# Clustered attention and a SwiGLU FFN on one core: two copies, two casts, two transposes and three weight loads change engine or place

## The chip, the cores and the metric

The kernel runs on one core of a Trainium2 chip. The core's engines work side by side, each through its own queue in order: TensorE (PE in the profile; PEld is its weight load), VectorE (DVE), ScalarE (ACT), GpSimd (POOL) and SyncE (SP), which issues DMAs. The metric is the device time of one execution in microseconds (us); of several executions the median is quoted.

## The reference

Batch 4, 8 heads, 768 tokens, head size 64; then a gated FFN from 512 to 1536 and back.

```python
q_assign = argmax(einsum('bhsd,hcd->bhsc', q_n, c_n))     # nearest of 16 centroids
k_assign = argmax(einsum('bhsd,hcd->bhsc', k_n, c_n))
mask = q_assign[:, :, :, None] == k_assign[:, :, None, :]
scores = where(mask, scale * q @ k.T, -1e9)
attn = softmax(scores)
x = (attn @ v) -> (tokens, heads * head size)
xn = x / sqrt(mean(x * x) + 1e-6) * rms_g
out = (silu(xn @ w_gate) * (xn @ w_val)) @ w_out
```

Each query attends only to keys of its own cluster.

## The kernel before, in words

**Tiling.** Tokens lie on 128 partitions. Work goes by units: a unit is one batch entry and one half of its queries (384), so there are 8 units of 8 heads. A head's scores take three steps of 384 queries by 256 keys, each followed by one exponential. A place (u, h, i) names unit, head and step; the steps of the first unit are also counted as gaps 0 to 23 (gap 3h + i). Heads are gathered in groups of four: group 0 is heads 0 to 3 of the first batch entry, group 1 heads 4 to 7, group 2 and 3 the next entry's.

**The mask.** Queries and keys are extended by 16 rows that hold the one-hot code of their cluster. A key's code is part of the product, so that scores of the same cluster rise by a large constant, which the exponential's bias takes away again; the others become zero.

**A head's preparation.** `trans` transposes a head's queries or keys on TensorE into a PSUM tile (`tq`), which VectorE or ScalarE copies to SBUF (`qkT`), as its argument says. `cast` turns one half of such a copy into bf16 in `qext` or `kext` (K0, K1, Q0, Q1 are the halves of keys and queries). `pair_clusters(p)` makes the one-hot codes of heads 2p and 2p + 1: products with the centroids on TensorE (`sc`), then a block transpose, a maximum and a comparison on VectorE (`scT`, `mx`, `pads`). `head(n)` lays head n's codes under keys and queries by two block transposes on VectorE (`under`). `vcast` turns a head's values into bf16 on GpSimd.

**Attention.** `scores` makes a step's products and its exponential on ScalarE (`pT`). `pv` multiplies a head's exponentials by its values. Two heads share one accumulator (`acc`, one buffer); behind the second of them VectorE divides by the row sums (`inv`, `x`), and only then may the next pair use the accumulator. In `attention`, step 1 of head h is followed by `pv` of head h - 1.

**Order.** The schedule is written by hand: what is emitted first stands first in its engine's queue. In the first unit the table `first` says what is emitted in which gap, behind that gap's scores and `pv`: gap 1 `gap1` (codes of heads 2 and 3, casts of heads 4 and 5), gaps 2 to 4 the transposes of heads 6 and 7 (`early`), gap 5 `gap5` (codes of heads 4 and 5, casts and value casts on GpSimd, two weight loads, at its end `head(4)`), gap 7 `head(5)`, gap 9 codes of heads 6 and 7, gap 10 `head(6)`, gap 13 the casts of head 6's keys and `head(7)`, from gap 15 transposes of group 2 (`late`). Gaps without an entry get `more`: one filler matmul (`warm`). All of `tq`, `sc`, `warm` and the FFN's products share one PSUM tag (`gen`) with three buffers, taken in turn.

In the second unit the FFN of the first one is mixed with the preparation of the next batch entry. `prep` is a list of such steps: `c` (value casts and loads), `a` (codes of group 2 and their placing by small DMAs on SP's queue), then transposes `t3` and casts `c3` of group 3, woven one by one; `spread` puts the three loads of the output weights `wo` (`o3`, on GpSimd's queue) evenly between them.

Of the kernel before, what the change touches and what calls it, by code (L numbers as in the profile page):

```python
# [22 lines left out]
def kernel(  # L23
# [12 lines left out]
    nc = tc.nc  # L36
# [48 lines left out]
    def load_qk(n):  # L85
        if n < B * H:
            load(n, 0)
            load(n, 1)

    def load_v(n, vq=None):  # L90
        if n >= B * H:
            return
        stagedv[n] = stage.tile([P, ST, D], F32, tag="vs", name="vs", bufs=NV)
        (vq or nc.sync).dma_start(out=stagedv[n], in_=src(v, n))
# [18 lines left out]
    def busy(n, first=True):  # L113
        to = ps_a.tile([P, 512], F32, tag="acc", name="warm") if first else \
            ps_g.tile([P, 512], F32, tag="gen", name="warm")
        for i in range(n):
            nc.tensor.matmul(to.rearrange("p (a b) -> p a b", b=P), lhsT=warm,  # L117
                             rhs=warm.unsqueeze(1).broadcast_to([P, 4, P]), start=True, stop=True)
# [72 lines left out]
    def load_gv(i):  # L191
        c = slice(i * DF // 4, (i + 1) * DF // 4)
        for w, of in ((wg, moe_w_gate), (wv, moe_w_val)):
            nc.gpsimd.dma_start(out=w[:, :, c], in_=of[:, c].rearrange("(c p) f -> p c f", p=P))

    def load_o(c):
        nc.gpsimd.dma_start(out=wo[:, c:c + 4], in_=moe_w_out[c * P:(c + 4) * P].rearrange("(c p) f -> p c f", p=P))
# [4 lines left out]
    def trans(g, h, part, on=None):  # L202
        if (g, h // 2) not in qkT:
            qkT[g, h // 2] = qk32.tile([P, 2, 2, UQ], F32, tag="qkT", name="qkT")
        qk = staged[g * HG + h]
        ps = ps_g.tile([P, UQ], F32, tag="gen", name="tq")
        for i in range(HT):
            nc.tensor.transpose(ps[:, i * P:(i + 1) * P], qk[:, part, 2 * i:2 * i + 2].rearrange("p t d -> p (t d)"),  # L208
                                ident_f)
        to, by = qkT[g, h // 2][:, h % 2, part], 1.0 / ZS if part else 1.0  # L210
        if on is nc.vector:
            nc.vector.tensor_scalar_mul(to, ps, by)
        else:
            nc.scalar.activation(to, ps, ACT.Copy, scale=by)  # L214
# [5 lines left out]
    def cast(on, g, h, part, es=(0, 1)):  # L220
        for e in es:
            to = cols((kext if part else qext)[g % 4][:D, h], g, e)
            of = qkT[g, h // 2][e * D:(e + 1) * D, h % 2, part]
            if on is nc.scalar:
                nc.scalar.copy(to, of)
            else:
                on.tensor_copy(to, of)  # L227

    def vcast(n):
        nc.gpsimd.tensor_copy(vbf[n // HG % 4][:, n % HG, :, :D], stagedv[n])  # L230
# [62 lines left out]
    def slot(n, m):  # L293

        return 32 * (2 * (n % 2) + m if n < 2 else 2 * m + n % 2)

    def pair_clusters(p, heads=(0, 1)):
        g, h = divmod(2 * p, HG)
        what = [(h + i, m) for i in heads for m in range(2)]
        at = [slot(2 * p + i, m) for i in heads for m in range(2)]  # L300
        r = slice(min(at), max(at) + 32)
        pool = ps_g if p else ps_s
        ps = pool.tile([P, UQ], F32, tag="gen" if p else "s", name="sc")
        for a, (hh, m) in sorted(zip(at, what)):
            nc.tensor.matmul(ps[a:a + 32], lhsT=cblk[:, g * HG + hh], rhs=qkT[g, hh // 2][:, hh % 2, m],
                             start=True, stop=True)
        sct = asg.tile([P, UQ], F32, tag="scT", name="scT", bufs=2)
        nc.vector.transpose(sct[r], ps[r])
        cl = sct[r].rearrange("p (b e c) -> p b e c", e=2, c=NC)
        mx = small.tile([P, NB, 2], F32, tag="mx", name="mx")[r]  # L310
        nc.vector.tensor_reduce(mx, cl, axis=AX, op=ALU.max)
        nc.vector.tensor_tensor(pads[p][r, :, :NC].rearrange("p b c e -> p b e c"), cl,  # L312
                                mx.unsqueeze(3).broadcast_to([mx.shape[0], NB, 2, NC]), op=ALU.is_equal)

    def under(n, m):
        i = slot(n, m)
        nc.vector.transpose((kext if m else qext)[n // HG][D:D + 32, n % HG].bitcast(I32),  # L317
                            pads[n // 2][i:i + 32].rearrange("p b c e -> p (b c e)").bitcast(I32))
# [181 lines left out]
    def weave(t, c):  # L500

        return [x for pair in zip(t, c) for x in pair] + c[len(t):]
# [5 lines left out]
    def spread(a, b):  # L508

        if not a:  # L510
            return list(b)
        w, n = [], 0
        for i, x in enumerate(a):
            w.append(x)
            while n < len(b) * (i + 1) // len(a):
                w.append(b[n])
                n += 1
        return w

    def ffn_work(u):  # L520
        n = UNITS[u][2] / HT
        w = [(0.18 * n, lambda c=c: xtrans(u, c)) for c in range(CC)]
        for f in range(FC):
            for val in (False, True):
                w.append((0.64 * n, lambda f=f, val=val: gv(u, f, val)))
        return w

    def out_work(u):
        return [(0.86, lambda t=t, p=p: out_mm(u, t, p)) for t in range(UNITS[u][2]) for p in range(3)]
# [10 lines left out]
    def head(n):  # L540
        under(n, 1)
        under(n, 0)

    def casts(on, n, *what):
        for m, e in what:
            cast(on, n // HG, n % HG, m, (e,))

    K0, K1, Q0, Q1 = (1, 0), (1, 1), (0, 0), (0, 1)
    pool_ = nc.gpsimd
# [32 lines left out]
    def more():  # L582
        busy(1, False)
# [3 lines left out]
    def second_batch():  # L587
        nc.sync.dma_start(out=hold, in_=invs[0].rearrange("p a t -> p (a t)"))
        for n in range(H + HG, H + NQ):
            load_qk(n)  # L590
        for n in range(H, H + NV):
            load_v(n)
# [13 lines left out]

    def gap5():
        pair_clusters(2)
        casts(pool_, 6, Q0)
        vcast(4)  # L610
        casts(pool_, 7, Q0)
        for n in (4, 5):
            casts(pool_, n, Q1)
        vcast(5)
        casts(pool_, 7, K0, K1)
        vcast(6)
        load_gv(2)
        vcast(7)
        for n in (6, 7):
            casts(pool_, n, Q1)  # L620
        load_gv(3)
        head(4)

    early = [lambda h=h, m=m: trans(1, h, m) for h in (2, 3) for m in (1, 0)]
    late = [lambda h=h, m=m: trans(2, h, m, nc.vector if h < 3 else None) for h in range(HG) for m in (1, 0)]
    first = {0: lambda: trans(1, 0, 0), 1: gap1, 2: early[0], 3: early[1], 4: lambda: (early[2](), early[3]()), 5: gap5,
             7: lambda: head(5), 9: lambda: pair_clusters(3), 10: lambda: head(6),
             13: lambda: (casts(nc.vector, 6, K0, K1), head(7)), 14: lambda: (more(), second_batch())}
    first.update({16: None, 19: None, 22: None})
    first.update({i: f for i, f in zip((15, 17, 18, 20, 21, 23), late)})  # L630

# [24 lines left out]
    for u in range(1, NU):  # L656
        ffn, o, g = ffn_work(u - 1), out_work(u - 2) if u > 1 else [], u + 2
        if u == 1:
            t, c, a = group_work(2)
            t3, c3, a3 = group_work(3)  # L660
            n = LEAD - 4
            o3 = [(0.0, lambda i=i: load_o(i)) for i in range(0, FC, 4)]
            prep = c + a + spread(weave(t3[n:], c3), o3) + a3[:5]
            idle = const.tile([P, 1], BF16)

            def norm():
                rms(0)
                nc.gpsimd.tensor_copy(idle, xn[0][:, HT - 1, DM - 1:])
                for h in range(HG):
                    casts(pool_, H + h, K0, Q0, K1, Q1)  # L670

            hooks = {(1, 0, 0): late[6], (1, 0, 1): lambda: (late[7](), norm())}
            hooks.update({(1, *divmod(2 + i, HT)): t3[i][1] for i in range(n)})
            hooks[1, *divmod(LEAD - 1, HT)] = lambda: xtrans_all(0)
            fill = spread(ffn[CC:CUT], prep)
            attention([(1, h) for h in range(H)], fill, LEAD, hooks)
        else:
            fill = ffn_work(u - 2)[CUT:] + [(0.0, lambda u=u: rms(u - 1))]
            fill += border(spread(o[:3], a3[5:]) + o[3:], ffn) if u == 2 else border(o, ffn)
            attention([(u, h) for h in range(H)], fill + spread(ffn[CC:CUT], group(g) if g < NG else []), 1)  # L680
# [41 lines left out]
```

The softmax here doesn't subtract the row's maximum and nothing guards it: scores larger than these inputs give would overflow.

## Time and profile before

| | us |
|---|---|
| median of 9 runs | 347.2 |
| lowest and highest | 347.05, 353.47 |
| the profiled execution, its time | 353.47 |
| its span | 351.7 |
| TensorE busy | 340.8 (97%) |
| ScalarE busy | 260.0 (74%) |
| VectorE busy | 221.3 (63%) |
| GpSimd busy | 113.0 (32%) |

The profiled execution is one of the nine, and the longest. Its span runs from the first to the last instruction; the remaining 1.8 us lie around it. Times in the text that name a moment are microseconds from the span's start.

The page gives busy time in 40 slices of 8.8 us, as tenths; the fourth row is the TensorE clock that was granted:

```profile
PE   8999999599999999999999999999999999999996
DVE  6999796748457745686457863677456653666330
ACT  5899979455787877887688877978778887764422
POOL 6999596210542702444033711427000000000000
PEclk9999999879999999999999999999999999999999
```

The first four slices are the first attention unit. The eighth slice (62 to 70 us) is the only one before the last where TensorE is much less than full, and the clock is lower there and in the slice behind it.

### The profile page before, as it was taken

The page shows a single profiled execution, that of the slowest core. Times are in us where ns is not written, and L with a number is a line of the kernel's source. Part 1 is how long each engine was busy: PE and PEld are TensorE (multiplying, and loading weights), DVE is VectorE, ACT ScalarE, POOL GpSimd, SP SyncE. Part 2 cuts the span into 40 slices and gives each one's busy share as a digit, 9 for nine tenths or more (in the row PEclk, how much of TensorE's full clock was granted, in tenths as well). Part 3 has the DMA queues.
Part 4 walks back from the last instruction along what each step waited for, and adds up shares of the span by engine and source line. Part 5 has one row for each costly group of instructions (what it writes and reads, how often), then busy time and mean ns, then how long its engine had stood idle before and what let it go on. Part 6 is the DMA issues. An engine that isn't in the chain of part 4 may idle for free.

```text
span 351.7 us, 7999 instructions
## 1 busy us (share of the span) xinstructions
PE 340.8 (97%) x3045; PEld 209.6 (60%) x3045; DVE 221.3 (63%) x540; ACT 260.0 (74%) x449; POOL 113.0 (32%) x225
## 2 busy tenths in 40 slices
PE   8999999599999999999999999999999999999996
PEld 4547657264665656655576556756566656665654
DVE  6999796748457745686457863677456653666330
ACT  5899979455787877887688877978778887764422
POOL 6999596210542702444033711427000000000000
PEclk9999999879999999999999999999999999999999
DMA  7999979762262012610130011000010001001002
GB/s 277 372 200 209 267 146 235 122 213 100 71 183 90 23 62 91 187 34 17 60 122 2 17 38 60 2 2 23 32 62 0 2 31 62 2 1 62 30 2 89
DMA packets 27302, 31.62 MB, mean 90 GB/s; under 512 B 4480, under 2 KB 24320, under 8 KB 27264
## 3 DMA queue, kind: packets, MB, share of 16 engines
q1 hardware_dynamic: 18608, 25.02, 21.6%
q0 software_dynamic: 8368, 5.71, 10.1%
q8 instruction: 24, 0.39, 0.5%
q10 hardware_dynamic: 288, 0.39, 0.3%
q14 instruction: 14, 0.11, 0.1%
HBM read 28.35 MB, written 6.29 MB: 98 GB/s over the span
## 4 chain that ended last, share of the span: by engine, by line
PE 82%; ACT 6%; DVE 5%; DMA 5%; issue 1%; POOL 0%; ACTq 0%; DVEq 0%; POOLq 0%
PE o L448 17%; PE gate L423 16%; PE val L423 16%; PE s L333 15%; PE acc L351 9%; ACT pT L337 4%; PE tq L208 4%; PE sc L241 2%; DMA kext<-oh 2%; DMA qk<-in_q_dram 2%; PE tx L396 1%; PE warm L117 1%; DVE pads L312 1%; DVE kext L317 1%; DVE qext L317 1%
## 5 line engine op out<-in xcount | busy, mean ns | idle before, releaser
L337 ACT ACTIVATE pT<-s,off 128x768 bf16<-128x768 f32 x192 | 170.9, 905 | 38.7 <-PE s L333 37.9
L333 PE MATMUL s<-qext,kext 80*128 80x384 bf16 x384 | 95.0, 329 | 5.8 <-DMA kext<-oh 3.9
L432 DVE SCALAR_TENSOR_TENSOR th<-th,gate 128x384 f32<-128x384 f32 x84 | 46.4, 552 | 54.3 <-ACT th L431 54.2
L423 PE MATMUL gate<-xnT,wg 128*128 128x384 bf16 x384 | 79.3, 328 | 0.5 <-DVE gvT L436 0.4
L423 PE MATMUL val<-xnT,wv 128*128 128x384 bf16 x384 | 78.8, 328 | 0.0
L448 PE MATMUL o<-wo,gvT 128*128 128x512 bf16 x276 | 67.4, 379 | 0.0
L227 POOL CAST qext<-qkT 64x384 bf16<-64x384 f32 x64 | 35.4, 559 | 76.2 <-ACT qkT L214 67.9
L333 PEld LDWEIGHTS <-kext 80*128 80x128 bf16 x384 | 36.5, 98 | 36.3 <-issue 11.1
L431 ACT ACTIVATE th<-gate 128x384 f32<-128x384 f32 x84 | 41.2, 491 | 15.5 <-PE gate L423 15.1
L423 PEld LDWEIGHTS <-wv 128*128 128x128 bf16 x384 | 36.3, 98 | 25.6 <-issue 4.3
L423 PEld LDWEIGHTS <-wg 128*128 128x128 bf16 x384 | 36.2, 98 | 25.6 <-issue 4.5
L436 DVE SCALAR_TENSOR_TENSOR gvT<-th,val 128x384 bf16<-128x384 f32 x84 | 46.2, 550 | 6.5 <-PE val L423 2.0
L351 PEld LDWEIGHTS <-pT 128*128 128x128 bf16 x1152 | 43.9, 98 | 10.2 <-DVE x L358 1.1
L351 PE MATMUL acc<-vbf,pT 128*128 128x65 bf16 x1152 | 46.2, 194 | 0.6 <-ACT pT L337 0.2
L448 PEld LDWEIGHTS <-gvT 128*128 128x128 bf16 x276 | 25.8, 97 | 25.1
L208 PE MATMUL tq<-ident_f,qk 128*128 128x128 f32 x192 | 31.2, 282 | 0.1
L214 ACT ACTIVATE qkT<-tq 128x384 f32<-128x384 f32 x57 | 26.9, 495 | 4.2 <-PE tq L208 3.7
L282 POOL DMA_DIRECT2D qext<-oh x40 | 19.2, 488 | 30.6 <-DVE oh L271 30.6
L397 DVE TENSOR_SCALAR xnT<-tx,gcol 128x384 bf16<-128x384 bf16 x28 | 10.5, 412 | 28.8 <-PE tx L396 28.8
L208 PEld LDWEIGHTS tq<-ident_f,qk 128*128 128x128 f32 x192 | 24.0, 145 | 6.8 <-ACT qkT L214 1.0
L451 ACT COPY o_sb<-o 128x512 f32<-128x512 f32 x23 | 13.5, 586 | 17.4 <-PE o L448 17.4
L282 POOL DMA_DIRECT2D kext<-oh x40 | 19.1, 487 | 15.8 <-DVE oh L271 15.8
(81 smaller groups left out, 247.9 us busy)
## 6 DMA issues: line engine op xcount, KB each, us to landing
qk<-in_q_dram SPq DMA_DIRECT2D x32, 192.0 KB, 3.7
vs<-in_v_dram SPq DMA_DIRECT2D x32, 192.0 KB, 4.0
out_dram<-o_sb SPq DMA_DIRECT2D x23, 256.0 KB, 2.0
qk<-in_k_dram SPq DMA_DIRECT2D x30, 192.0 KB, 3.9
wg<-in_moe_w_gate_dram POOLq DMA_DIRECT2D x4, 384.0 KB, 8.6
wv<-in_moe_w_val_dram POOLq DMA_DIRECT2D x4, 384.0 KB, 10.8
wo<-in_moe_w_out_dram POOLq DMA_DIRECT2D x3, 512.0 KB, 9.2
qext<-oh POOLq DMA_DIRECT2D x40, 12.0 KB, 1.6
```

The costliest lines, as they stand in the source:

```text
L208: nc.tensor.transpose(ps[:, i * P:(i + 1) * P], qk[:, part, 2 * i:2 * i + 2].rearrange("p t d -> p (t d)"), ident_f)
L214: nc.scalar.activation(to, ps, ACT.Copy, scale=by)
L227: on.tensor_copy(to, of)
L282: on.dma_start(out=ext[D:D + NC, h, e * UQ:(e + 1) * UQ], in_=put[g, m][32 * h + e * NC:32 * h + (e + 1) * NC])
L333: nc.tensor.matmul(ps[:, j, :w] if nt == HT else flat[:, j * w:(j + 1) * w], lhsT=cols(kext[g % 4][:KR, hh], g, kc // HT, kc % HT * P, (kc ...
L337: nc.scalar.activation(pT[u, h][:, n * i:n * i + n, :w], of, ACT.Exp, bias=off, scale=scale * ZS)
L351: nc.tensor.matmul(acc[:, h % 2, t], lhsT=pT[u, h][:, kc, t * P:(t + 1) * P], rhs=vbf[g % 4][:, hh, kc % HT * 2 + kc // HT], start=kc == 0 ...
L423: nc.tensor.matmul(ps, lhsT=w[:, c, f * P:(f + 1) * P], rhs=xnT[u][:, c, :n], start=c == 0, stop=c == CC - 1)
L431: nc.scalar.activation(th, ps, ACT.Tanh, scale=0.5)
L432: nc.vector.scalar_tensor_tensor(th, th, 1.0, ps, op0=ALU.add, op1=ALU.mult)
L436: nc.vector.scalar_tensor_tensor(gvT[u][:, f, :n], gates[u], 0.5, ps, op0=ALU.mult, op1=ALU.mult)
L448: nc.tensor.matmul(outs[u], lhsT=gvT[u][:, f, t * P:(t + 1) * P], rhs=wo[:, f], start=f == 0, stop=f == FC - 1)
```

## The change

- The transposes of head 7 are copied out of PSUM by VectorE instead of ScalarE.
- The casts of both halves of head 6's keys leave VectorE in gap 13 and stand on GpSimd in gap 5, behind the first half of head 6's queries.
- `head(4)` moves from the end of gap 5 to gap 7, ahead of `head(5)`. In gap 7 the `pv` of head 1 and its division are emitted before it.
- The first six of the 14 woven steps of group 3 get no output weight load between them; the three loads are spread over the other eight.

```diff
     def gap5():
         pair_clusters(2)
-        casts(pool_, 6, Q0)
+        casts(pool_, 6, Q0, K0, K1)
         vcast(4)
...
         load_gv(3)
-        head(4)
 
-    early = [lambda h=h, m=m: trans(1, h, m) for h in (2, 3) for m in (1, 0)]
+    early = [lambda h=h, m=m: trans(1, h, m, nc.vector if h > 2 else None) for h in (2, 3) for m in (1, 0)]
...
-             7: lambda: head(5), 9: lambda: pair_clusters(3), 10: lambda: head(6),
-             13: lambda: (casts(nc.vector, 6, K0, K1), head(7)), 14: lambda: (more(), second_batch())}
+             7: lambda: (head(4), head(5)), 9: lambda: pair_clusters(3), 10: lambda: head(6),
+             13: lambda: head(7), 14: lambda: (more(), second_batch())}
...
-            prep = c + a + spread(weave(t3[n:], c3), o3) + a3[:5]
+            w = weave(t3[n:], c3)
+            prep = c + a + w[:6] + spread(w[6:], o3) + a3[:5]
```

## The prediction

> **What bounds the kernel now.** I read, in this order, the chain of waits from the start to 75 us, the timelines of VectorE, ScalarE, TensorE and GpSimd from 10 to 45 us, and the busy time by stretches. From about 40 us on TensorE is full (the stretches 40 to 56, 80 to 90, 100 to 110 and 110 to 200 us show it busy for all of their length), and its own work isn't changed. So the change can act in two places: the first attention unit, up to 40 us, and the one hole behind it, at 66 to 70 us.
>
> In the first place VectorE has no hole from 7.25 to 35 us. Its timeline, cut to the lines used here:
> ```profile
> 18.48 0.58 DVE L308 STREAM_TRANSPOSE scT<-sc 128x384 f32<-128x384 f32 x1
> ...
> 20.42 0.57 DVE L317 STREAM_TRANSPOSE kext<-pads 32x384 int32<-32x384 int32 x1
> 21.00 0.57 DVE L317 STREAM_TRANSPOSE qext<-pads 32x384 int32<-32x384 int32 x1
> 21.61 0.20 DVE L356 RECIPROCAL inv<-acc 128x6 f32<-128x6 f32 x1
> 21.84 0.56 DVE L358 TENSOR_TENSOR x<-acc,inv 128x384 f32<-128x384 f32 x1
> 22.42 0.57 DVE L317 STREAM_TRANSPOSE kext<-pads 32x384 int32<-32x384 int32 x1
> ...
> 26.71 0.20 DVE L356 RECIPROCAL inv<-acc 128x6 f32<-128x6 f32 x1
> 26.94 0.56 DVE L358 TENSOR_TENSOR x<-acc,inv 128x384 f32<-128x384 f32 x1
> 27.41 1.08 DVE L227 CAST kext<-qkT 64x384 bf16<-64x384 f32 x2
> 28.53 0.57 DVE L317 STREAM_TRANSPOSE kext<-pads 32x384 int32<-32x384 int32 x1
> 29.11 0.57 DVE L317 STREAM_TRANSPOSE qext<-pads 32x384 int32<-32x384 int32 x1
> 29.71 1.49 DVE L212 TENSOR_SCALAR qkT<-tq 128x384 f32<-128x384 f32 x3
> ```
> Each line begins where the one before ends. 20.42 is head 4's one-hots, 22.42 head 5's; the two divisions (21.61, 26.71) free the single accumulator `acc`, for heads 2 and 3, and then for heads 4 and 5. The chain of waits shows what hangs on the second:
> ```profile
> 26.94 0.57 DVE x L358
> 27.50 0.05 issue
> 27.55 0.72 PE acc L351 x18
> 28.27 0.36 PE s L333 x2
> 28.63 0.02 issue
> 28.65 0.69 ACT pT L337
> ```
> The attention product of head 4 starts 0.05 us behind the division, scores (0,5,2) stand behind it in TensorE's queue, and their exponential starts at 28.65. From there ScalarE does eight exponentials in a row up to 35.1 us, the last product follows, then the norm (VectorE from 35.02 to 39.65) and the first FFN transposes. ScalarE has only 0.18 us of idle time before 28.65: **whatever makes the second division late moves all that follows.**
>
> **Head 7's copies on VectorE.** They leave ScalarE (two at 17.32, 0.89 us together, done by 18.2) and stand on VectorE behind head 3's one-hots, which end at 18.45. The row for such a copy is the last line of the first fence: three in 1.49 us, of 0.55 each, so a spacing of 0.47. Two take 0.94 us. Nothing leaves VectorE between 18.45 and 26.71, and it has no hole there, so the second division moves from 26.71 to 27.65 and `x` ends at 28.44 instead of 27.50: **+0.94 us**. What ScalarE gains: exponential (0,1,2) can start at about 17.35 instead of 18.06. That gain ends at once. In gap 6 TensorE has a filler matmul ("warm") whose PSUM slot is that of head 7's key transpose (three slots, taken in turn). It was free for the filler at 18.38; now it waits for the first VectorE copy, to 18.48 + 0.55 = 19.03, and behind it stand scores (0,2,1), which started at 19.05 and now start at about 19.25. Their exponential comes at 19.8 instead of 19.7. So the relief of ScalarE is worth nothing by gap 8.
>
> **Head 4's one-hots behind the division.** Two transposes of 0.57 (1.18 with their issue) change places with a division of 0.8. The first division was to be at 21.61; with 0.94 added and 1.18 taken from ahead of it, it starts at 21.37, and `x` ends at 22.16 instead of 22.40. The product of head 2 and the exponential behind it come 0.24 us earlier (23.3 for 23.55). The one-hots of head 4 end at 22.16 + 1.18 = 23.34; scores (0,4,0) ran at 23.57, so they just make it. Sum to the second division: zero, as both orders lie ahead of it. The 0.24 is then idle time of ScalarE before 28.65.
>
> **Head 6's keys on GpSimd.** VectorE loses the line at 27.41, 1.08 us, but this lies behind the second division. Head 7's one-hots therefore end at 29.60 instead of 29.68, and the copies behind them are on time: no gain on the chain. GpSimd gets two casts in front of these:
> ```profile
> 26.31 0.50 POOL L230 CAST vbf<-vs 128x384 bf16<-128x384 f32 x1
> ...
> 29.03 0.51 POOL L230 CAST vbf<-vs 128x384 bf16<-128x384 f32 x1
> 29.48 1.29 POOL L227 CAST kext<-qkT 64x384 bf16<-64x384 f32 x2
> ```
> Price, by the nearest row (29.48, the same form beside a busy VectorE): 1.29 us for two; the bounds are 1.0 (0.50 each, as at 40 us) and 1.7 (0.79 and more, as at 28.17). Against this stands the Trainium skill, "GPSIMD Engine Reference", section Engine selection, by which one-input work runs at about line rate there, while its Key points hold that GpSimd shares SBUF interfaces with VectorE. Line rate, for which I take the undisturbed 0.50, gives 1.0; the row gives 1.3. I take the row. Queued behind are: values of head 4 (ready at 26.8, now 28.1; needed by the delayed product at 28.49), values of head 5 (29.54, now 30.83; needed at 29.94 + 0.94 = 30.88), keys of head 7 (30.77, now 32.06; needed at 31.19 + 0.94 = 32.13), then weight loads at 31.29 and 35.0, whose columns the FFN doesn't read in this unit's first microseconds. GpSimd then idles 3.3 us before 39.8. All three are covered, but only by VectorE's delay: with no delay there, GpSimd alone would cost 28.1 - 27.55 = 0.55 to 0.9 us. At 1.7 for the pair the keys would be 0.3 late, of which 0.14 is slack before their exponential.
>
> **Output weights put off.** Each piece is cut in a list of 14 steps: loads came behind step 5, 10, 14, now behind 9, 12, 14. On GpSimd only some steps have work (steps 2, 6, 10, 13), so just the first load passes one of them: it moves from 51.84 behind the cast and value cast of group 3's second head, to about 53.8. The second and third keep their place (57.48, 61.08). The cast that it lets past (52.66) waits for ScalarE's copy ending at 52.6 anyway: nothing gained. SP's queue keeps its order. What it can touch is this hole (stretches: us, then PE, PEld, DVE, ACT, POOL busy, then clock, DMA share, GB/s):
> ```profile
> 64.00:72.00 8.00, 4.06 (x39) 2.20 (x32) 4.26 (x12) 2.90 (x4) 3.83 (x8) 0.74 0.54 91
> 72.00:80.00 8.00, 8.00 (x57) 4.71 (x56) 3.89 (x8) 4.45 (x7) 0.05 (x1) 0.83 0.81 267
> ```
> TensorE waits 3.94 us for the one-hots of group 2's keys, whose eight small transfers stand on SP behind loads while the weights share the DMA engines. Behind it matmuls run at half speed: four of "gate" take 1.28 us for 0.65, and over the groups up to 74.7 that is 2.2 us. Together 6.1 us. The profiled execution took 353.47 us (span 351.7) and the median run 347.2: the 6.27 between them is this hole, so I take it that the median run hasn't got it. Then the value for the median is 0; the bounds are -1 (a share of the hole is there too: a load 1.9 us later, at about half of the DMA engines, lets SP's transfers land some 0.9 earlier) and +2 (the load collides with the small transfers instead). For the changed kernel's profile: by the row alone the hole shrinks to 3.0; by "TensorE: Matmul & The Clock Gate", Part 1, where the clock falls after about 3.4 us idle, the 2.2 us would go as well, 3.1 in all. No run here shows which.
>
> **Sum.** 0.94 - 0 + 0 + 0 = +0.94, made against a span that, without the hole, is 345.4: 347.2 + 0.94 = **348.1 us**.
>
> **Rivals.**
> - ScalarE is the bound of the first unit (it is busy 11.37 of 11.55 us from 23.55), and 0.98 us fewer copies bring it all forward. It decides if the fillers don't wait and the division keeps its time. 347.2 - 0.98 = 346.2. Against it: the 0.57 us wait for `x` at 27.55, and a full VectorE.
> - Covered: VectorE's operations get shorter where the others move (the comparison took 0.60 to 0.87 for one form), and GpSimd's casts likewise: 347.2 to 347.6.
> - The hole at 66 us opens in ordinary runs: first load and small transfers collide. 347.2 + 0.94 + 2 to 6 = 350 to 354. For it: the small transfers took 5 to 7 us to land. Against: eight unprofiled runs within 347.05 to 347.40, so some margin.
>
> **Numbers.** Forecast 0.60 (347.7 to 348.8), ScalarE 0.12, covered 0.16, hole 0.12. A measurement here can tell 0.2% from no change, 0.7 us. Faster 0.11; within 0.22 (covered, and the low end of the forecast); slower 0.67. Range 346.6 to 349.4: it leaves out half of the ScalarE case and the hole.
>
> **What would show it.** In the changed profile: VectorE's two copies at about 18.5; the filler of gap 6 at 19.0; first division at 21.4, second at 27.65; head 4's product at 28.5 with VectorE as releaser; the eight exponentials from 29.6; the norm's end near 40.6. I am wrong if the second division stands at 26.7 or earlier, if GpSimd's values or keys release TensorE last, or if the 66 us hole decides the median.

## The result and the profile after

The changed kernel takes 349.82 us in the median (347.97 to 350.29), the kernel before 347.19: a ratio of 1.007, 95% interval 1.006 to 1.0079. That is 2.63 us slower; 0.94 was forecast, and 349.82 lies above the range. The profiled execution is one of the shorter ones: 348.61 us, span 346.8. Executions more than 1.5% above the fastest of the same kernel are left out of the ratios here and below (four of the kernel before, at 353 to 1224 us, one with head 4's move alone, at 578 us, and two of the kernel before with head 6's one-hots behind, at 353 us); what slowed those above 354 us is not known.

From the page of the changed kernel, the engines in 40 slices of 8.7 us; the eighth slice is full now, and the page has no clock row: its mean clock is 1.00:

```profile
span 346.8 us, 7999 instructions
...
PE   7998999999999999999999999999999999999996
...
DVE  6999787975578645786267854687456554675330
ACT  5898979865887768887787877978778877764422
POOL 6999596244344403371041801436000000000000
```

The stretches of the changed kernel where the hole was (us, then PE, PEld, DVE, ACT, POOL busy, clock, DMA share, GB/s):

```profile
64.00:72.00 8.00, 7.99 (x81) 4.78 (x80) 7.19 (x20) 6.33 (x10) 2.73 (x6) 1.00 0.77 143
72.00:80.00 8.00, 8.00 (x79) 4.39 (x77) 6.20 (x24) 5.01 (x7) 1.15 (x3) 1.00 0.84 284
```

TensorE is busy for 7.99 of 8.00 us at full clock: this execution has no hole. Its span is nevertheless longer than the 345.4 that the span before would have without one, and the excess lies in the first unit. VectorE's timeline of the changed kernel (start, duration, instruction):

```profile
18.00 0.57 DVE L317 STREAM_TRANSPOSE qext<-pads 32x384 int32<-32x384 int32 x1
18.60 1.02 DVE L212 TENSOR_SCALAR qkT<-tq 128x384 f32<-128x384 f32 x2
19.54 0.57 DVE L308 STREAM_TRANSPOSE scT<-sc 128x384 f32<-128x384 f32 x1
...
20.73 0.92 DVE L312 TENSOR_TENSOR pads<-scT,mx 128x384 bf16<-128x384 f32 x1
21.55 0.18 DVE L356 RECIPROCAL inv<-acc 128x6 f32<-128x6 f32 x1
...
25.96 0.99 DVE L312 TENSOR_TENSOR pads<-scT,mx 128x384 bf16<-128x384 f32 x1
...
28.40 0.56 DVE L358 TENSOR_TENSOR x<-acc,inv 128x384 f32<-128x384 f32 x1
```

Start-up differs by a few tenths between executions, so I count from the end of head 3's one-hots (18.45 before, 18.57 here). The second `x` ends 10.39 us behind that point and not 9.05: **1.34 us late**. The two copies take 0.94 of it, as forecast (18.60 to 19.54). The two comparisons take 0.92 and 0.99 us; the same two before took 0.64 and 0.60, so 0.67 more. The gaps behind the two comparisons are 0.27 shorter: 0.20 behind the first, where the division now starts on the comparison's heels and a one-hot transpose had to wait for its end, and 0.07 behind the second. The chain of waits of the changed kernel at this place:

```profile
28.40 0.57 DVE x L358
28.97 0.05 issue
29.01 0.72 PE acc L351 x18
29.73 0.36 PE s L333 x2
30.09 0.02 issue
30.12 0.69 ACT pT L337
```

It is the chain of before link by link, 1.34 us later against head 3's one-hots (10.44 for 9.10 at the product). This explains the profiled execution: 348.61 is 1.42 above the old median. It doesn't explain the other 1.2 us of the median. These go with the granted clock: of 17 executions of the changed kernel (11 here, 6 in the first experiment) five had a clock of 0.999 or 1.00 and took 347.90 to 348.77; twelve had 0.994 or 0.995 and took 349.39 to 350.47.

### The profile page after: what moved, and what is told of

Its sections match the earlier page's. It is cut to its first block, busy times and chain, and to the rows that moved or that the text cites. A ratio compares the mean times of both kernels' runs of the same rounds, so it can differ in the third digit from the quotient of the medians.

```text
span 346.8 us, 7999 instructions
## 1 busy us (share of the span) xinstructions
PE 337.5 (97%) x3045; PEld 207.7 (60%) x3045; DVE 222.3 (64%) x540; ACT 259.2 (75%) x447; POOL 113.8 (33%) x227
## 4 chain that ended last, share of the span: by engine, by line
PE 84%; DVE 7%; ACT 6%; issue 1%; DMA 1%; ACTq 0%; DVEq 0%
PE o L448 17%; PE gate L423 17%; PE val L423 17%; PE s L333 15%; PE acc L351 9%; ACT pT L337 4%; PE tq L208 4%; PE sc L241 3%; PE tx L396 1%; DVE pads L312 1%; DVE kext L317 1%; DVE qext L317 1%; DMA c_in<-in_centroids_dram 1%; DVE scT L308 1%; DVE mx L311 1%
## 5 line engine op out<-in xcount | busy, mean ns | idle before, releaser
L208 PE MATMUL tq<-ident_f,qk 128*128 128x128 f32 x192 | 30.3, 275 | 0.1
L214 ACT ACTIVATE qkT<-tq 128x384 f32<-128x384 f32 x55 | 25.9, 494 | 3.9 <-PE tq L208 3.6
L208 PEld LDWEIGHTS tq<-ident_f,qk 128*128 128x128 f32 x192 | 23.1, 141 | 7.2 <-ACT qkT L214 1.0
```

## The experiments

Twelve kernels, all timed beside the kernel before, whose median was 347.12, 347.28 and 347.16 in the three groups (a, b, c). The columns "x ends" and "product" count from the end of head 3's one-hots in the profiled execution; "wait" is TensorE's wait just ahead of head 4's product; a clock of 1.00 stands for 0.999 too.

| kernel | x ends | product | wait | clock of its runs | median | ratio (95%) |
|---|---|---|---|---|---|---|
| before | 9.05 | 9.10 | 0.17 | 1.00 | 347.12 to 347.28 | |
| changed (first experiment) | 10.37 | 10.43 | 1.59 | 0.995 in 4 of 6 | 349.70 | 1.0063 (1.0044 to 1.0083) |
| copies alone | 10.33 | 10.38 | 0.30 | 1.00 | 348.18 | 1.0032 (1.0020 to 1.0044) |
| casts alone | 9.02 | 9.72 | 0.80 | 1.00 | 347.87 | 1.0027 (1.0018 to 1.0037) |
| weights alone | 9.04 | 9.10 | 0.16 | 1.00 | 347.01 | 0.9996 (0.9988 to 1.0005) |
| head 4 alone | 8.85 | 8.90 | 0.23 | 1.00 | 346.98 | 0.9998 (0.9989 to 1.0006) |
| changed, no copies | 8.86 | 9.56 | 0.89 | 1.00 | 347.47 | 1.0010 (1.0003 to 1.0017) |
| changed, six fillers | 10.38 | 10.43 | 0.29 | 1.00 | 348.26 | 1.0033 (1.0021 to 1.0045) |
| changed, two fillers | 10.37 | 10.42 | 1.15 | 1.00 | 348.23 | 1.0035 (1.0022 to 1.0047) |
| changed, head 4 back | 10.38 | 10.44 | 0.36 | 1.00 | 348.35 | 1.0033 (1.0021 to 1.0045) |
| changed, head 6 behind | 9.06 | 9.45 | 0.39 | 1.00 | 347.37 | 1.0007 (0.9999 to 1.0015) |
| before, head 6 behind | 8.17 | 9.01 | none | see below | 347.67 | 1.0010 (1.0001 to 1.0019) |
| one copy | 7.96 | 8.44 | none | 1.00 | 346.91 | 0.9995 (0.9987 to 1.0004) |

### The changed kernel again

No edit.

> The changed kernel once more, for another profile and the granted clock of its runs. Theory (second division late): 1.4 us of its excess are the second division, 28.2 for 26.7, and the product of head 4 behind it; the remaining 1.2 us of the median come from TensorE's clock: its wait of 1.6 us for that division makes the throttle fall to half speed there in most runs. Then runs near 349.8 show a clock near 0.995, runs near 348.5 show 1.00, and a profile that shows a lower clock has it between 28 and 36 us. Rival (the hole at 66 us): the lower clock, if the profile catches it, lies at 66 to 75 us behind a wait for the small transfers of group 2's codes.

The profile caught an execution with the lower clock (349.53 us). TensorE's timeline of this kernel, then its stretches (us, PE, PEld, DVE, ACT, POOL busy, clock, DMA share, GB/s):

```profile
26.41 0.50 PE L333 MATMUL s<-qext,kext 80*128 80x384 bf16 x2
28.50 1.03 PE L351 MATMUL acc<-vbf,pT 128*128 128x65 bf16 x18 [1.59 <-DVE x L358]
29.34 0.83 PE L333 MATMUL s<-qext,kext 80*128 80x384 bf16 x2
29.96 0.84 PE L208 MATMUL tq<-ident_f,qk 128*128 128x128 f32 x3
30.60 0.85 PE L333 MATMUL s<-qext,kext 80*128 80x384 bf16 x2
```

```profile
28.50:30.00 1.50, 1.50 (x21) 1.24 (x22) 1.46 (x3) 0.00 (x0) 1.44 (x4) 0.57 0.34 43
30.00:31.00 1.00, 1.00 (x6) 0.77 (x5) 0.37 (x2) 0.80 (x1) 0.91 (x2) 0.50 0.77 266
31.00:32.00 1.00, 1.00 (x6) 0.85 (x5) 0.40 (x1) 0.56 (x2) 0.97 (x2) 0.50 0.38 106
32.00:33.00 1.00, 1.00 (x22) 0.78 (x21) 0.56 (x1) 0.91 (x2) 1.00 (x3) 0.94 0.89 292
```

TensorE waits 1.59 us for `x`, and the clock is at half from 28.71 us, 0.2 us behind the end of this wait, to 32.12 us. The product takes 1.03 us for 0.72, a pair of scores 0.83 for 0.51. ScalarE, which sets the pace here, is idle for the whole of 28.5 to 30.0 and again behind its first exponential. At 66 us nothing is lost: the rival is out, and the place is the one that the theory named.

The lengths show more. From its first rise the clock is at full for 23.89 us and then at half for 3.41. In the profile before it is at full for 61.44 us and at half for 6.82 (67.87 to 74.69, behind the hole). The kernel before with head 6's one-hots behind, below, has 64.85 and 3.41 us (69.84 to 73.25). All six are whole multiples (7, 1, 18, 2, 19, 1) of 3.413 us: in these traces the clock changes only at moments that far apart. These are the stretch between two such moments that ends at the fall, and the one behind it (columns as above):

```profile
25.30:28.71 3.41, 1.76 (x16) 0.90 (x15) 3.23 (x7) 2.69 (x4) 3.26 (x7) 1.00 1.07 164
28.71:32.12 3.41, 3.41 (x28) 2.67 (x25) 2.01 (x4) 1.48 (x2) 3.22 (x6) 0.50 0.51 130
```

The first holds the whole wait, and TensorE is busy for 1.76 of its 3.41 us. In the stretches ahead of the other two falls it is busy for 1.66 and 0.99 us. Eleven of the fourteen profiles have a record of the clock; counted off in such stretches, none shows it staying at full behind a stretch with less than 2.00 us (this profile, 342.74 to 346.15).

### Each part alone

Copies alone: the line of `early` from the diff. Casts alone: the two lines with `casts`. Weights alone: the two lines of `prep`. Head 4 alone: the two lines with `head(4)`.

> The kernel before with head 7's two copies on VectorE and nothing else. Theory: the second division comes 0.94 us later by the copies, more if the comparisons meet GpSimd's casts: 348.1 to 348.6, and 349.5 if the longer wait lowers TensorE's clock. Rival (hole at 66 us by the later weight load): 348.1 with a clock as before. Rival (ScalarE is the bound): 346.2.

> The kernel before with the casts of head 6's keys on GpSimd and nothing else. My prediction's reading: the values of head 4 come at 28.1, the product of head 4 waits for them and not for the division, +0.55 to +0.9 us: 347.8 to 348.1. Rival (a comparison on VectorE that starts just behind a cast waits for it): the comparison of heads 6 and 7 starts at 24.81 as before, ahead of the casts, and keeps its 0.60 us; if it is longer, this kernel is slower by that as well.

> The kernel before with the output weights put off and nothing else. Theory: no effect on the median, 347.2 within 0.2, as the hole at 66 us isn't in ordinary runs; in the profile the small transfers of group 2's codes are issued about 1 us earlier. Rival (the later load collides with these transfers): 348 to 350, with a lower clock.

> The kernel before with head 4's one-hots behind the first division and nothing else. Theory and prediction: no effect, 347.1 to 347.4, as the same work lies ahead of the second division; the first product comes some tenths earlier and the wait for the second division grows by as much.

All four came out within or close to what was expected: +1.06, +0.75, -0.11 and -0.18 us against the group's median of before, the last two not distinguishable from none. With the copies alone the comparisons took 0.93 and 0.78 us; with the casts alone 0.62 and 0.59, so the rival for the casts is out, and the wait is the one for head 4's values (timeline of TensorE, casts alone):

```profile
28.07 0.71 PE L351 MATMUL acc<-vbf,pT 128*128 128x65 bf16 x18 [0.80 <-POOL vbf L230]
```

With the weights alone the issue of the eight small transfers of group 2's keys ended at 63.1 us; with head 4's move alone, whose weights are where they were, at 64.7. In these two profiles the transfers behind the later load are 1.6 us earlier, but in an execution without the hole nobody waits for them. The parts do not add up to the change: 1.06 + 0.75 - 0.11 - 0.18 is 1.5, and the median rose by 2.6.

### The changed kernel with fillers in the wait

```diff
                 for p in due:
+                    if p == (0, 4):
+                        busy(6, False)
                     pv(*p)
...
-             ... 14: lambda: (more(), second_batch())}
+             ... 14: second_batch}
```

`busy(6, False)` emits six filler matmuls.

> The changed kernel with six filler matmuls (0.21 us each, 1.3 us) ahead of head 4's product, where TensorE waits 1.6 us for the second division, in place of the one filler of gap 14. The division is as late as before. Theory (delay plus clock): the clock stays at 1.00 in all runs, the median falls from 349.8 to 348.5 (within 0.3), and no run is above 349.2. Rival (the delay alone): the median stays at 349.7 or goes up by a few tenths through the fillers.

> The changed kernel with two fillers ahead of head 4's product instead of six: TensorE's wait for the second division is then about 1.15 us, between the 1.07 us of the kernel with head 4's one-hots back (clock 1.00) and the 1.6 us of the changed kernel (0.995 in most runs). If the clock falls only for waits nearer to 1.6 us: 348.3 and 1.00. If it depends on where the wait falls in a window that runs free of the program: a mixture, with runs at 348.3 and at 349.8.

TensorE's timeline with six fillers:

```profile
26.95 1.46 PE L117 MATMUL warm<-warm 128*128 128x512 bf16 x6
28.70 0.72 PE L351 MATMUL acc<-vbf,pT 128*128 128x65 bf16 x18 [0.29 <-DVE x L358]
```

The division is as late as in the changed kernel (10.38), yet all five executions keep a clock of 1.00 and take 348.04 to 348.56. The delay alone would have left the median at 349.7. So the second half of the loss is the clock, and it follows from the length of the wait. Two fillers (the same edit with `busy(2, False)`) are enough: with a wait of 1.15 us five of five executions keep the clock. TensorE's timeline with two fillers, then a stretch of it:

```profile
29.03 0.72 PE L351 MATMUL acc<-vbf,pT 128*128 128x65 bf16 x18 [1.15 <-DVE x L358]
```

```profile
27.41:30.82 3.41, 2.26 (x30) 1.56 (x28) 3.25 (x8) 1.81 (x3) 3.24 (x7) 1.00 0.63 101
```

In this profile the clock rose at 6.93 us; six times 3.413 us later this stretch begins. It holds the whole wait, TensorE is busy for 2.26 us of it, and the clock stays. A wait of 1.6 us leaves less, 1.76 us in the kernel above, when it lies whole between two of the moments at which the clock can change, and more when one of them cuts it. That would be why only some executions of the changed kernel lose the clock. It is read from the profiles, not tested: no run moved the wait against these moments, and the profile of the changed kernel that kept its clock has no record of them.

### The changed kernel with head 4's one-hots back

The two lines with `head(4)` as before the change.

> The changed kernel with head 4's one-hots ahead of the first division again. Theory: the second division is as late as in the changed kernel (the same work lies ahead of it), but TensorE waits in two places, over 1 us for the first division and about 0.3 us for the second, so no single wait is long: the clock stays at 1.00, 348.3 to 348.7. Rival (where the one-hots stand is nothing to the clock): 349.7 with 0.995 in most runs.

TensorE's timeline of this kernel, the products of head 2 and of head 4:

```profile
23.46 0.72 PE L351 MATMUL acc<-vbf,pT 128*128 128x65 bf16 x18 [1.07 <-DVE x L358]
...
28.76 0.72 PE L351 MATMUL acc<-vbf,pT 128*128 128x65 bf16 x18 [0.36 <-DVE x L358]
```

The second division is late by the same amount, but TensorE waits in two pieces, 1.07 and 0.36 us, and the clock stays: 348.35. So the move of head 4's one-hots, which is worth nothing alone, costs 1.4 us here: it lets TensorE and ScalarE run ahead of the first division, and the whole delay then falls into a single wait at the second.

### Head 6's one-hots behind the second division

```diff
-             ... 10: lambda: head(6),
-             13: lambda: head(7), ...
+             13: lambda: (head(6), head(7)), ...
```

For the kernel before, gap 13 becomes the casts, `head(6)`, `head(7)`. Gap 10 has no entry then and gets a filler.

> The changed kernel with head 6's one-hots (two transposes, 1.2 us) moved from gap 10 to gap 13, behind the second division. Theory: this division comes 1.2 us earlier, head 4's product then waits for its values on GpSimd until about 28.0 (from a start at which head 3's one-hots end at 18.45), some 0.4 us later than in the kernel before; clock 1.00; 347.5 to 347.8. Rival (GpSimd's longer list or something behind 30 us decides): above 348.2.

> The kernel before with head 6's one-hots moved behind the second division and the casts. Theory: the 0.18 us of idle time of ScalarE before its eight exponentials go, and no more, as ScalarE is full on both sides: 346.9 to 347.1, which can hardly be told from 347.1. If the second division were the only bound it would be 1.2 us: 346.0.

In the changed kernel, moving 1.2 us of VectorE's work from ahead of the second division takes away 2.3 us: `x` ends at 9.06, as before the change, and what is left is GpSimd's (TensorE's timeline):

```profile
27.54 0.71 PE L351 MATMUL acc<-vbf,pT 128*128 128x65 bf16 x18 [0.39 <-POOL vbf L230]
```

347.37 is slightly below the 347.5 expected, and not distinguishable from the kernel before. In the kernel before the same move didn't help: 347.67 instead of 346.9 to 347.1. ScalarE does fourteen exponentials in a row, as expected, but the first of them comes 0.25 us later, behind the filler that I had let into gap 10. Three of its fifteen executions took 352 to 353 us; the profile caught one of these (TensorE's waits from 64 to 72 us: in total, times, longest):

```profile
PE s L333 <- DMA kext<-oh: 2.4, 1, 2.4
```

This is the hole of the profile before. It opens in some executions of the old order of loads; of the first nine of the kernel before, in one.

### The changed kernel without the copies

> The changed kernel with head 7's copies on ScalarE again (so: casts on GpSimd, head 4's one-hots behind the division, weights put off). Theory: the second division is as early as in the kernel before, head 4's product waits for its values on GpSimd as with the casts alone, some 0.6 to 0.8 us in all: 347.8 to 348.1; TensorE's wait is about 1.0 us and the clock stays at 1.00. Rival (the place of the one-hots lowers the clock by itself): 349 with 0.995.

The line of `early` as before the change. The product waits 0.89 us for head 4's values and starts 0.46 us late, the clock is 1.00 or 0.999. The median rose by 0.31, less than the 0.6 to 0.8 expected; GpSimd's two casts ahead of the added ones took 1.31 us here for the 1.50 with the casts alone.

### An attempt at a faster kernel

```diff
-    early = [... trans(1, h, m, nc.vector if h > 2 else None) ...]
+    early = [... trans(1, h, m, nc.vector if h > 2 and m == 0 else None) ...]
...
-        casts(pool_, 6, Q0, K0, K1)
+        casts(pool_, 6, Q0)
         vcast(4)
+        casts(pool_, 6, K0, K1)
         casts(pool_, 7, Q0)
-        for n in (4, 5):
-            casts(pool_, n, Q1)
...
         vcast(6)
+        for n in (4, 5):
+            casts(pool_, n, Q1)
```

The casts of Q0 stay ahead of `vcast(4)`, and head 6's one-hots stand behind the second division.

> An attempt at a faster kernel: only head 7's queries are copied by VectorE, head 6's one-hots stand behind the second division, its key casts on GpSimd behind head 4's values, the second query halves of heads 4 and 5 later; head 4's one-hots and the weights as in the change. Theory: the second division ends some 0.5 us earlier than in the kernel before, nothing on GpSimd is late, ScalarE has 0.4 us less to do: 346.7 to 346.9. Rival (the first unit is full on all engines): 347.1 or above.

346.91 against 347.16, ratio 0.9995 with an interval from 0.9987 to 1.0004: as expected in size, but not told from no change. ScalarE's timeline shows why it isn't more:

```profile
23.09 11.28 ACT L337 ACTIVATE pT<-s,off 128x768 bf16<-128x768 f32 x14 [0.21 <-PE s L333]
35.19 0.49 ACT L214 ACTIVATE qkT<-tq 128x384 f32<-128x384 f32 x1 [0.83 <-POOL qext L227]
```

The product of head 4 is 0.66 us earlier than before, and fourteen exponentials run without a gap. Then ScalarE stands idle for 0.83 us ahead of its next copy, waiting for the query casts that I had put off on GpSimd; before, it stood 0.32 us there. No version beat the kernel before measurably.

## Why the prediction was right or wrong

**The bound** was right for a second division that comes later: in the changed kernel, one move of 1.2 us of other work across it changed the median by 2.3 us. An earlier one gained nothing: in the kernel before, the same move brought `x` forward by 0.88 us but head 4's product by 0.09, and the median was 347.67.

**Head 7's copies**: the mechanism was right, the size was not. The copies cost 0.94, measured 0.94, and the filler of gap 6 waited for the first of them, 0.53 us where 0.65 was forecast. What failed is the step "Two take 0.94 us. Nothing leaves VectorE between 18.45 and 26.71 ... so the second division moves ... +0.94 us". It held all other durations fixed. The two comparisons behind the copies went from 0.64 and 0.60 to 0.92 and 0.99. I had the spread of 0.60 to 0.87 in hand and used it only for the covered rival, as a possible gain. The timelines of both kernels show what it follows. Before, VectorE's comparisons and GpSimd's casts beside them:

```profile
19.68 0.64 DVE L312 TENSOR_TENSOR pads<-scT,mx 128x384 bf16<-128x384 f32 x1
...
24.81 0.60 DVE L312 TENSOR_TENSOR pads<-scT,mx 128x384 bf16<-128x384 f32 x1
```

```profile
19.83 1.61 POOL L227 CAST kext<-qkT 64x384 bf16<-64x384 f32 x2
...
24.86 1.52 POOL L227 CAST qext<-qkT 64x384 bf16<-64x384 f32 x2
```

After, GpSimd's casts, to be held against the comparisons at 20.73 and 25.96:

```profile
19.97 1.29 POOL L227 CAST kext<-qkT 64x384 bf16<-64x384 f32 x2
...
25.94 1.45 POOL L227 CAST kext<-qkT 64x384 bf16<-64x384 f32 x2
```

Before, each comparison started 0.15 or 0.05 us ahead of a cast, and that cast was long (0.93 and 0.99 us, against 0.61 for others of the form). After, a cast had started just ahead of the comparison, by 0.08 us (the second of the pair at 19.97) or 0.02, and the comparison was long. A cast that is further on costs it less: in the kernel with one copy it had started 0.31 us ahead of the first comparison, which took 0.69. In all six kernels with both copies the first comparison took 0.91 to 0.93 and the second 0.78 to 1.00; in the kernels with one copy or none, 0.62 to 0.69 and 0.59 to 0.60. The comparison has two SBUF operands, which is the case for which the Trainium skill, "GPSIMD Engine Reference", Key points, states contention with GpSimd; the size and the dependence on who starts first are from these runs. That the start order is the cause is read from the traces; no run shifted a cast by itself.

**Head 4's one-hots**: "Sum to the second division: zero" was right for the division, which came 0.2 us earlier with this part alone. That the time gained ahead "is then idle time of ScalarE" was right too; together with the delay it comes to 1.62 us in the changed kernel. But I didn't ask what TensorE's idle time does to its clock.

**The clock** is the other step that failed, and the larger part of the miss: some 1.2 of the 1.69 us between forecast and median, where the comparisons, less the shorter gaps, are 0.40. The prediction weighed it only for the hole at 66 us, and by the skill's rule: "TensorE: Matmul & The Clock Gate", Part 1, lets the clock fall after at least one idle window of about 3.4 us. By that rule a wait of one to two microseconds is harmless. The runs decide against it: behind waits of 1.6 us the clock fell in 12 of 17 executions, behind waits of up to 1.15 us in none of those that the ratios count. The length agrees with the 3.41 us measured, but the stretch need not be idle: TensorE was busy for 1.76 us of it. It costs 1.3 us: the median of the twelve is 349.9, that of the five others 348.6.

**Head 6's keys on GpSimd**: right. Alone 0.55 to 0.9 was forecast and 0.75 measured, with the releaser named; beside the copies it is covered, since the kernel with six fillers (348.26) has them and takes no more than the copies alone (348.18).

**Output weights**: right. Nothing for the median (347.01), and the hole was not in the median run.

**ScalarE as the bound**: out. The copies alone, which leave ScalarE less to do, made the kernel 1.06 us slower.

## What to carry to other kernels

When an instruction is added to a full engine, look at what its neighbours will now run beside: two comparisons that lost their place ahead of GpSimd's casts cost 0.67 us, on top of 0.94 us for the work added. Sum up where waits will gather. An edit that lets TensorE run ahead of a result was free alone here; with the result late it turned two waits of 1.1 and 0.4 us into one of 1.6, behind which the clock fell in 12 of 17 executions, to half for 3.4 us in the profile; two filler matmuls in the wait kept it at full.

## What the runs showed of the hardware

TensorE's clock fell to half behind a wait of only 1.6 us, for 3.41 us, and not in every execution of the same program. With the same lateness and a wait of 1.15 us it never fell in five executions. In the profiles the clock changes only at moments a multiple of 3.413 us apart; it fell where TensorE had been busy for 1.76 us or less of the 3.41 before such a moment, and stayed where it had been busy for 2.00 or more. Where between the two it turns stays open, and so does whether the place of the wait between these moments is what lets five of 17 executions escape. A comparison on VectorE with two SBUF operands and a cast on GpSimd that start within 0.16 us of each other lengthen each other: the one that started second took 0.2 to 0.4 us more. This too is read from the traces and not tested by itself.
